# Block with sliding-window attention and a gated MLP: one tile for a stack's queries, one for its keys, in place of one for each half of the tokens

## The chip, the cores and the metric

One NeuronCore of a Trainium2 chip. The metric is the device time of one execution in microseconds, as the median of several runs. Each kernel also leaves one profiled execution, on which all the traces rest: the instructions of TensorE (PE, its weight loads PEld), VectorE (DVE), ScalarE (ACT), GpSimd (POOL) and the DMA queue of SyncE (SP), with their waits.

## The reference

Sequence S = 2048, width D = 640, all float32. The block is attention and then a gated MLP, each behind a layer norm and with a residual; the change touches the attention alone.

```python
H = 32; Dh = D // H; W = 256                       # Dh = 20
q, k, v = split(layernorm(x) @ wqkv)               # [H, S, Dh] each
scores = einsum("bhqd,bhkd->bhqk", q, k) * Dh ** -0.5
mask = (i - j >= 0) & (i - j < W)                  # query i, key j
p = softmax(where(mask, scores, -1e9))
h = x + (einsum("bhqk,bhkd->bhqd", p, v)) @ wo
z1, z2 = split(gelu(layernorm(h) @ w_in)); z2 = layernorm(z2)
h2 = h + (z1 * (w_sp @ z2 + b_sp)) @ w_out
```

Each query sees itself and the 255 keys before it. A block of 128 keys meets the 384 queries that begin with it; a block of 128 queries meets the 384 keys that end with it.

## The kernel before

**Stages.** First layer norm and the values (`vgemm`), then the query and key projections (`qk_item`) with the first maxima between them (the dense stage, to about 238 us), then the sliding attention in *units* (238 to about 457 us), the output projection, and the MLP.

**Stacks.** 32 heads are worked in 8 stacks of 4 heads. Queries and keys are split into three bf16 parts each, so that six products of parts stand for one float32 product; the six products are stacked along the contraction: 6 x 20 = 120 rows. Rows 120 to 122 hold ones on the side of the keys, and on the side of the queries the three bf16 parts of minus the row maximum, so that the same matmul with 123 rows yields score minus maximum. The projections write the parts to DRAM (`qk_d`, laid out by half of the heads, part, half of the tokens b, then rows, heads and 1024 tokens), and `load_stack` (L326 to L344) brings a stack back into SBUF with 24 DMAs: for each half b of the tokens, each of six products j and each side a (0 queries, 1 keys), 20 rows of 4 heads x 1024 tokens, 160 KB. A stack has a *slot* of two tiles of 16 KB a partition; three slots (0 and 1 of their own, 2 inside the buffer xb) are used in turn, `g % 3`. In the code before, tile b of a slot holds queries and keys of token half b, `p (a h t)`: so a row of one load is one run of 8 KB in SBUF. `slot_ap` views the tiles as bf16 for the matmuls, `slot_w` as float32 words of two tokens for the DMAs and memsets.

**Units.** Unit u is stack g = u // 16, key block kb = u % 16; NU = 128. In the loop over s (L788), unit s's scores (`score_item`), the maxima of unit s + 18 (`max_item`, LEAD = 18) and the PV products of unit s - 2 (`pv_item`) are interleaved head by head, for hh in 0 to 3.

- `max_item` (L359): scores of one head for 128 queries, without the maximum, in four strips of 32 queries (`tile_position` puts strip j on its own 32 columns of the array), each against the 288 keys that it can see (L373). Three PSUM banks (`ring[1]`) are used in turn; DVE takes the masked maximum of the bank (L383). Units below 18, in the dense stage, use one matmul of 128 queries and up to 384 keys (L377). After eight units, `max_rows` transposes the maxima on PE (L389), splits them into bf16 parts on DVE and POOL (L392 to L396), stores them (L398) and loads them into rows 120 to 122 of the queries (L400).
- `score_item` (L405): four strips of 32 keys against 288 queries each (L426) into one of three other banks; ACT takes the exponential (L429, in the last units L431), POOL zeroes what the window excludes (L433, L436).
- `pv_item` (L439): 16 matmuls (L454), copies from PSUM by ACT (L473) or DVE (L475), a store (L476).

**Where the halves meet.** A strip whose moving tokens lie on both sides of token 1024 takes them from two tiles, so `tokens` (L346) cuts it, and each piece becomes a matmul with a weight load of its own. That is so for maxima of query blocks 8 and 9 and for scores of key blocks 6 and 7 of every stack.

**Loads in time.** `load_stack(G)` starts when stack G - 2's scores start and issues one load in even units and two in odd ones, so it is spread over that stack's 16 units, with half 0 ahead of half 1 (for stack 0: queries ahead of keys). Stack G's maxima start in the last two of these 16 units with half 0; half 1 is first needed in key block 6 of stack G - 1.

**Order.** SP's, PE's, DVE's and ACT's instructions run in the order of the program throughout the attention; POOL's from unit 13 on is planned by the framework with a simulated time, and so is a part of the gate stage. Semaphores and waits follow from the tiles that each instruction reads and writes.

Of the kernel before, what the change touches and what calls it, by code (L numbers as in the profile page):

```python
# [7 lines left out]
F32 = mybir.dt.float32  # L8
# [7 lines left out]
P = 128  # L16
# [18 lines left out]
def block_kernel(ctx, tc, x, xt, wqk, wv, wo, w_in, wsp, bsp, w_out, out):  # L35
# [226 lines left out]
    with ExitStack() as ab:  # L262
# [19 lines left out]

        def add_slot(i, halves):

            slot_ap[i] = [h.bitcast(BF16).rearrange("p (a h t) -> p a h t", a=2, h=4) for h in halves]
            slot_w[i] = [h.bitcast(F32).rearrange("p (a h t) -> p a h t", a=2, h=4) for h in halves]

        add_slot(0, s0)
        add_slot(2, [h[:, :2 * S] for h in xb])
# [36 lines left out]
        def load_stack(g):  # L326


            st = slot_w[g % 3]
            if g < 2:  # L330
                for h in st:
                    nc.gpsimd.memset(h[96:P, 1], ONES)
            if g == 2:
                for h, ones in zip(st, slot_w[0]):
                    nc.sync.dma_start(h[120:123, 1], ones[120:123, 1])
                    yield
            parts = ((0, 0), (0, 1), (0, 2), (1, 0), (1, 1), (2, 0))
            loads = [(b, j, a) for b in range(2) for j in range(6) for a in range(2)]
            if g == 0:
                loads.sort(key=lambda load: load[2])  # L340
            for b, j, a in loads:
                src = qk_d[g // 4, parts[j][a], b, a * DH:(a + 1) * DH, g % 4 * 4:g % 4 * 4 + 4]
                nc.sync.dma_start(st[b][j:6 * DH:6, a], src)
                yield  # L344

        def tokens(st, rows, a, hh, t0, n):  # L346

            o = 0
            while o < n:
                c, t = divmod(t0 + o, S // 2)  # L350
                w = min(n - o, S // 2 - t)
                yield o, w, st[c][:rows, a, hh, t:t + w]
                o += w

        def one(st, rows, a, hh, t0, n):
            (_, _, x), = tokens(st, rows, a, hh, t0, n)
            return x

        def max_item(g, qb, hh, strips=True):  # L359

# [5 lines left out]
            if strips:  # L366
                skip = 32 if qb > 1 else 0
                if skip:
                    n, keep = 288, strip
                for j in range(4):  # L370
                    q0 = qb * P + 32 * j
                    for o, w, k in tokens(st, 120, 1, hh, lo + skip * j, n):
                        nc.tensor.matmul(ps[32 * j:32 * j + 32, o:o + w], one(st, 120, 0, hh, q0, 32), k,  # L373
                                         start=True, stop=True, tile_position=(0, 32 * j))
            else:
                for o, w, k in tokens(st, 120, 1, hh, lo, n):
                    nc.tensor.matmul(ps[:, o:o + w], one(st, 120, 0, hh, qb * P, P), k, start=True, stop=True)  # L377
            b, c = divmod(qb, 8)
            if c == 0 and hh == 0:
                m_cols[g, b] = tmp2.tile([P, 32], F32, tag="mcol", bufs=2, name=f"mcol{g}_{b}")  # L380
# [5 lines left out]
        def max_rows(g, b):  # L386
# [10 lines left out]
            rows = m_d[g, b]  # L397
            nc.sync.dma_start(rows.rearrange("a r c -> r a c"), m3.bitcast(F32))  # L398
            yield
            nc.sync.dma_start(slot_w[g % 3][b][120:123, 0], rows.rearrange("a (h r) c -> a h (r c)", h=4))  # L400
            yield

        p_tiles, pv_tiles = {}, {}
# [1 line left out]
        def score_item(u, hh):  # L405
# [14 lines left out]
            for i in range(4):  # L420
                k0 = kb * P + 32 * i
                b, e = 32 * i, min(n, 32 * i + 288)
                if NU - NT < u and 4 * (u - NU + NT - 1) + hh < 6:
                    b, e = 0, n
                for o, w, q in tokens(st, 123, 0, hh, kb * P + b, e - b):
                    nc.tensor.matmul(ps[32 * i:32 * i + 32, b + o:b + o + w], one(st, 123, 1, hh, k0, 32), q,  # L426
                                     start=True, stop=True, tile_position=(0, 32 * i))
            if u <= NU - NT:
                nc.scalar.activation(pt[:, hh, :n], ps[:, :n], AF.Exp, scale=SCALE)  # L429
            elif hh % 2:  # L430
# [1174 lines left out]
```

## Time and profile before

| | |
|---|---|
| median of 3 runs | 1100.6 us (1099.38 to 1101.7) |
| profiled execution, its own time | 1096.99 us |
| granted TensorE clock | 1.0 |
| matmuls, weight loads | 11045 each |
| PE, DVE, ACT, POOL busy in the whole span | 1073.5, 779.6, 603.7, 308.9 us |
| DMA: packets, bytes | 92293, 194.78 MB |

PE's busy time is made of matmuls whose ends are modelled, and they overlap, so a busy PE can still be waiting between starts. "Idle before" in a group is time in which that engine did nothing ahead of the group's instructions, with what ended it; "issue" is an end that no semaphore explains. In a name such as `bank<-slot,slot` the output stands ahead of the arrow; `slot,slot` are the two tiles of a slot, `xb,xb` those of slot 2.

### The profile page before, as it was taken

Reading aid. Unit: us, or ns where it says so; the run is one execution under the profiler, and the core shown is the slowest. Engines: PE = TensorE matmul, PEld = TensorE weight load, DVE = VectorE, ACT = ScalarE, POOL = GpSimd, SP = SyncE. Lnnn points to the kernel's source line nnn. Section 1 sums busy time; section 2 is a strip of 40 time slices with the busy share of each in tenths; the row PEclk is TensorE's granted clock in tenths of the full one; section 3 lists DMA queues with packets and bytes.
Section 4 is the critical chain, followed back from the end, with each engine's and each line's share of the span. In section 5 each row is a group of like instructions: output and inputs, shape, how many; then the busy total and the mean of one; then the engine's idle time right before and its main releaser. Section 6 shows DMA issues by size and latency. Waiting matters only on the chain.

```text
span 1095.3 us, 28703 instructions
## 1 busy us (share of the span) xinstructions
PE 1073.5 (98%) x11045; PEld 967.9 (88%) x11045; DVE 779.6 (71%) x2157; ACT 603.7 (55%) x1257; POOL 308.9 (28%) x446
## 2 busy tenths in 40 slices
PE   8999999999999999999999999999999999999998
PEld 8998886668888787699999998999999899999998
DVE  6643445779999997586677678656556899988674
ACT  4444433249989899766766557433358433333331
POOL 4414445668766677622200012000001000000000
PEclk9999999999999999999999999999999999999999
DMA  7834566465665565679845342242341567684542
GB/s 257 296 117 118 174 212 217 150 214 174 191 186 184 187 192 172 193 217 289 316 179 186 113 135 77 71 142 87 126 150 51 176 230 249 231 280 139 181 156 97
DMA packets 92293, 194.78 MB, mean 178 GB/s; under 512 B 11958, under 2 KB 46278, under 8 KB 88262
## 3 DMA queue, kind: packets, MB, share of 16 engines
q1 hardware_dynamic: 92156, 192.95, 54.0%
q8 instruction: 87, 1.43, 0.5%
q14 instruction: 50, 0.41, 0.1%
HBM read 127.90 MB, written 64.95 MB: 176 GB/s over the span
## 4 chain that ended last, share of the span: by engine, by line
PE 84%; DMA 4%; issue 4%; ACT 3%; DVE 2%; POOL 1%; SPq 1%; ACTq 0%; POOLq 0%; DVEq 0%
PE g L1217 23%; PE zb L1102 8%; PE pv L454 7%; PE bank L373 5%; PE bank L426 5%; PE qk L612 4%; PE qk L613 4%; PE qk L614 4%; PE out_x L1381 3%; PE zx L1042 2%; PE out_v L1381 2%; PE zv L1042 2%; PE zy L1042 1%; PE zw L1042 1%; PE bank L377 1%
## 5 line engine op out<-in xcount | busy, mean ns | idle before, releaser
L429 ACT ACTIVATE pt<-bank 128x384 f32<-128x384 f32 (+1 forms) x452 | 180.5, 486 | 14.5 <-PE bank L426 9.7
L1217 PE MATMUL g<-zl,aw 128*128 128x432 f32 x768 | 168.9, 357 | 1.0 <-ACT zl L864 1.0
L383 DVE CUSTOM_DVE_ANT_0 junk<-bank,strip 128x288 bf16<-128x288 f32 x392 | 155.8, 452 | 9.8 <-PE bank L373 5.6
L864 ACT ACTIVATE aw<-fx 128x512 fp32r<-128x512 f32 (+2 forms) x152 | 86.1, 587 | 128.4 <-DVE fx L858 53.6
L1217 PEld LDWEIGHTS g<-zl,aw 128*128 128x128 f32 x768 | 144.0, 188 | 7.4 <-ACT zl L864 1.4
L858 DVE TENSOR_TENSOR aw<-fx,aw 128x512 fp32r<-128x512 f32 (+2 forms) x152 | 95.7, 638 | 58.8 <-ACT aw L864 53.8
L454 PE MATMUL pv<-pt,v_sb 128*32 128x192 f32 (+3 forms) x1984 | 133.3, 322 | 2.9 <-POOL pt L433 1.2
L1217 PE MATMUL g<-ze,aw 128*128 128x432 f32 x576 | 132.6, 359 | 2.3 <-DVE row L858 2.3
L1217 PEld LDWEIGHTS g<-ze,aw 128*128 128x128 f32 x576 | 107.1, 188 | 9.0 <-DVE row L858 3.7
L433 POOL TENSOR_SCALAR_AFFINE_SELECT pt<-pt 128x512 f32<-128x512 f32 x128 | 82.6, 646 | 58.1 <-ACT pt L429 55.1
L426 PE MATMUL bank<-slot 123*32 123x288 bf16 (+8 forms) x1296 | 94.8, 273 | 1.0 <-ACT pt L429 0.6
L373 PE MATMUL bank<-slot 120*32 120x288 bf16 (+4 forms) x1248 | 91.6, 275 | 3.0 <-issue 2.8
L454 PEld LDWEIGHTS pv<-pt,v_sb 128*32 128x32 f32 x1984 | 64.1, 110 | 10.2 <-POOL pt L433 5.1
L436 POOL TENSOR_SCALAR_AFFINE_SELECT pt<-pt 128x512 f32<-128x512 f32 x112 | 71.0, 634 | 0.0
L426 PEld LDWEIGHTS <-slot 123*32 123x32 bf16 x1728 | 59.3, 96 | 11.5 <-issue 1.7
L858 DVE TENSOR_TENSOR row<-g,row 128x432 f32<-128x432 f32 x80 | 48.3, 603 | 21.3 <-PE g L1217 20.9
L373 PEld LDWEIGHTS <-slot 120*32 120x32 bf16 x1408 | 51.0, 95 | 14.0 <-issue 5.6
L383 DVE CUSTOM_DVE_ANT_0 junk<-bank,mask 128x384 bf16<-128x384 f32 (+2 forms) x120 | 51.4, 444 | 16.6 <-PE bank L377 14.7
L645 POOL TENSOR_TENSOR sg<-rest,sg 128x512 bf16<-128x512 f32 x39 | 45.6, 1169 | 57.7 <-ACT sg L644 45.2
L630 DVE TENSOR_TENSOR rest<-qk,std 128x512 f32<-128x512 f32 x36 | 24.8, 690 | 42.4 <-PE qk L614 41.2
L635 ACT ACTIVATE sg<-rest 128x512 bf16<-128x512 f32 x39 | 24.6, 631 | 54.1 <-DVE rest L630 52.3
L118 PE MATMUL wo_ps<-xb,xb 128*128 128x320 f32 x260 | 52.4, 311 | 0.5 <-DVE mvc L1496 0.5
(289 smaller groups left out, 2534.5 us busy)
## 6 DMA issues: line engine op xcount, KB each, us to landing
slot<-qk_d SPq DMA_DIRECT2D x144, 160.0 KB
fx<-wsp_in SPq DMA_DIRECT2D x32, 512.0 KB
qk_d<-sg SPq DMA_DIRECT2D x39, 384.0 KB
o_d<-ot SPq DMA_DIRECT2D x64, 128.0 KB
xb<-qk_d SPq DMA_DIRECT2D x48, 160.0 KB
fx<-hn_d SPq DMA_DIRECT2D x24, 320.0 KB
z_d<-row SPq DMA_DIRECT2D x16, 432.0 KB
g_d<-row SPq DMA_DIRECT2D x16, 432.0 KB
```

Source lines behind the costliest of these rows:

```text
L373: nc.tensor.matmul(ps[32 * j:32 * j + 32, o:o + w], one(st, 120, 0, hh, q0, 32), k, start=True, stop=True, tile_position=(0, 32 * j))
L383: nc.vector.tensor_tensor_reduce(out=junk[:, :n], in0=ps[:, :n], in1=keep, scale=1.0, scalar=NEG, op0=OP.add, op1=OP.max, accum_out=m_cols ...
L426: nc.tensor.matmul(ps[32 * i:32 * i + 32, b + o:b + o + w], one(st, 123, 1, hh, k0, 32), q, start=True, stop=True, tile_position=(0, 32 * i))
L429: nc.scalar.activation(pt[:, hh, :n], ps[:, :n], AF.Exp, scale=SCALE)
L433: nc.gpsimd.affine_select(out=pt[:, :, :P], in_=pt[:, :, :P], pattern=[[0, 4], [1, P]], base=0, channel_multiplier=-1, compare_op=OP.is_ge ...
L436: nc.gpsimd.affine_select(out=pt[:, :, 256:], in_=pt[:, :, 256:], pattern=[[0, 4], [-1, P]], base=-1, channel_multiplier=1, compare_op=OP. ...
L454: nc.tensor.matmul(ps[32 * hh:32 * hh + 32, a - 512 * c:b - 512 * c], v_sb[:, kb, v0:v0 + 32], pt[:, hh, a - kb * P:b - kb * P], start=fir ...
L858: (eng or nc.vector).tensor_tensor(out=out, in0=a, in1=b, op=op)
L864: nc.scalar.activation(out, a, AF.Copy)
L1042: nc.tensor.matmul(ps, a[x], b[:, y], start=start and m + x + y == 0, stop=stop and m == n - 1 and x == 1, skip_group_check=True)
L1102: nc.tensor.matmul(b[0][:, :HF], a[:, x, kk], win2[0][:, y, kk, h * HF:(h + 1) * HF], start=kk + x + y == 0, stop=kk == KD - 1 and x == 1)
L1217: nc.tensor.matmul(ps, w[m][:, x, k], zc[k][m][:, y], start=start and k + x + y == 0, stop=stop and k == 3 and x == 1, skip_group_check=True)
```

## The change

Tile 0 of a slot now holds the queries of all 2048 tokens and tile 1 the keys, `p (h t)`. So every strip is one matmul, `tokens` is gone, and `one` is a plain slice. The loads read the same parts of `qk_d` in the same order, but a row's four heads of 1024 tokens now land 4 KB apart in four runs of 2 KB. The rows with minus the maximum (L400) land in the same manner. The ones (rows 96 to 127 by memset for slots 0 and 1, copied for slot 2) are written in two pieces of two heads of the keys' tile, where they were one piece for each half.

```diff
--- before.py
+++ after.py
@@ -282,8 +282,8 @@

         def add_slot(i, halves):

-            slot_ap[i] = [h.bitcast(BF16).rearrange("p (a h t) -> p a h t", a=2, h=4) for h in halves]
-            slot_w[i] = [h.bitcast(F32).rearrange("p (a h t) -> p a h t", a=2, h=4) for h in halves]
+            slot_ap[i] = [h.bitcast(BF16).rearrange("p (h t) -> p h t", h=4) for h in halves]
+            slot_w[i] = [h.bitcast(F32).rearrange("p (h t) -> p h t", h=4) for h in halves]

         add_slot(0, s0)
         add_slot(2, [h[:, :2 * S] for h in xb])
@@ -328,11 +328,11 @@

             st = slot_w[g % 3]
             if g < 2:
-                for h in st:
-                    nc.gpsimd.memset(h[96:P, 1], ONES)
+                for b in range(2):
+                    nc.gpsimd.memset(st[1][96:P, 2 * b:2 * b + 2], ONES)
             if g == 2:
-                for h, ones in zip(st, slot_w[0]):
-                    nc.sync.dma_start(h[120:123, 1], ones[120:123, 1])
+                for b in range(2):
+                    nc.sync.dma_start(st[1][120:123, 2 * b:2 * b + 2], slot_w[0][1][120:123, 2 * b:2 * b + 2])
                     yield
             parts = ((0, 0), (0, 1), (0, 2), (1, 0), (1, 1), (2, 0))
             loads = [(b, j, a) for b in range(2) for j in range(6) for a in range(2)]
@@ -340,21 +340,11 @@
                 loads.sort(key=lambda load: load[2])
             for b, j, a in loads:
                 src = qk_d[g // 4, parts[j][a], b, a * DH:(a + 1) * DH, g % 4 * 4:g % 4 * 4 + 4]
-                nc.sync.dma_start(st[b][j:6 * DH:6, a], src)
+                nc.sync.dma_start(st[a][j:6 * DH:6, :, b * S // 4:(b + 1) * S // 4], src)
                 yield

-        def tokens(st, rows, a, hh, t0, n):
-
-            o = 0
-            while o < n:
-                c, t = divmod(t0 + o, S // 2)
-                w = min(n - o, S // 2 - t)
-                yield o, w, st[c][:rows, a, hh, t:t + w]
-                o += w
-
         def one(st, rows, a, hh, t0, n):
-            (_, _, x), = tokens(st, rows, a, hh, t0, n)
-            return x
+            return st[a][:rows, hh, t0:t0 + n]

         def max_item(g, qb, hh, strips=True):

@@ -369,12 +359,12 @@
                     n, keep = 288, strip
                 for j in range(4):
                     q0 = qb * P + 32 * j
-                    for o, w, k in tokens(st, 120, 1, hh, lo + skip * j, n):
-                        nc.tensor.matmul(ps[32 * j:32 * j + 32, o:o + w], one(st, 120, 0, hh, q0, 32), k,
-                                         start=True, stop=True, tile_position=(0, 32 * j))
+                    nc.tensor.matmul(ps[32 * j:32 * j + 32, :n], one(st, 120, 0, hh, q0, 32),
+                                     one(st, 120, 1, hh, lo + skip * j, n),
+                                     start=True, stop=True, tile_position=(0, 32 * j))
             else:
-                for o, w, k in tokens(st, 120, 1, hh, lo, n):
-                    nc.tensor.matmul(ps[:, o:o + w], one(st, 120, 0, hh, qb * P, P), k, start=True, stop=True)
+                nc.tensor.matmul(ps[:, :n], one(st, 120, 0, hh, qb * P, P), one(st, 120, 1, hh, lo, n),
+                                 start=True, stop=True)
             b, c = divmod(qb, 8)
             if c == 0 and hh == 0:
                 m_cols[g, b] = tmp2.tile([P, 32], F32, tag="mcol", bufs=2, name=f"mcol{g}_{b}")
@@ -397,7 +387,8 @@
             rows = m_d[g, b]
             nc.sync.dma_start(rows.rearrange("a r c -> r a c"), m3.bitcast(F32))
             yield
-            nc.sync.dma_start(slot_w[g % 3][b][120:123, 0], rows.rearrange("a (h r) c -> a h (r c)", h=4))
+            nc.sync.dma_start(slot_w[g % 3][0][120:123, :, b * S // 4:(b + 1) * S // 4],
+                              rows.rearrange("a (h r) c -> a h (r c)", h=4))
             yield

         p_tiles, pv_tiles = {}, {}
@@ -422,9 +413,9 @@
                 b, e = 32 * i, min(n, 32 * i + 288)
                 if NU - NT < u and 4 * (u - NU + NT - 1) + hh < 6:
                     b, e = 0, n
-                for o, w, q in tokens(st, 123, 0, hh, kb * P + b, e - b):
-                    nc.tensor.matmul(ps[32 * i:32 * i + 32, b + o:b + o + w], one(st, 123, 1, hh, k0, 32), q,
-                                     start=True, stop=True, tile_position=(0, 32 * i))
+                nc.tensor.matmul(ps[32 * i:32 * i + 32, b:e], one(st, 123, 1, hh, k0, 32),
+                                 one(st, 123, 0, hh, kb * P + b, e - b),
+                                 start=True, stop=True, tile_position=(0, 32 * i))
             if u <= NU - NT:
                 nc.scalar.activation(pt[:, hh, :n], ps[:, :n], AF.Exp, scale=SCALE)
             elif hh % 2:
```

## The prediction

> **What bounds the kernel now.** I read the page first, then the windows view for the stage that the diff touches (units 0 to 112 of the sliding attention, 238 to 434 us, and the units behind them), then PE's waits inside that stage.
>
> ```profile
> span 1095.3 us, 28703 instructions
> ```
>
> ```profile
> 238.00:434.00 196.00, 190.01 (x5722) 160.92 (x5724) 183.84 (x934) 181.73 (x474) 139.97 (x241) 1.00 0.59 184
> 434.00:458.00 24.00, 22.00 (x543) 14.34 (x542) 9.86 (x14) 22.49 (x38) 20.49 (x32) 1.00 0.66 182
> ```
>
> ```profile
> PE bank L373 <- issue: 3.4, 5, 1.6
> ```
>
> The window rows list the length, then PE, PEld, DVE, ACT and POOL busy, the clock, the DMA share and GB/s. In the long stage PE is busy 190.0 of 196 us, DVE 183.8, ACT 181.7: three engines in step, so a saving on one is worth only what the other two leave. In the last units ACT holds 22.5 of 24 us, so PE's saving there counts nothing. Most of PE's idle time is "issue": it waits for nothing the profile shows; L373 alone has five such waits, 3.4 us.
>
> **What the change removes.** A matmul whose tokens cross 1024 was two, each with its own weight load.
>
> ```profile
> L426 PEld LDWEIGHTS <-slot 123*32 123x32 bf16 x1728 | 59.3, 96 | 11.5 <-issue 1.7
> L373 PEld LDWEIGHTS <-slot 120*32 120x32 bf16 x1408 | 51.0, 95 | 14.0 <-issue 5.6
> L373 PEld LDWEIGHTS <-xb 120*32 120x32 bf16 x576 | 20.7, 95 | 5.2 <-issue 1.6 <-DMA xb<-qk_d 0.2
> L426 PEld LDWEIGHTS <-xb 123*32 123x32 bf16 x576 | 20.0, 96 | 3.5 <-issue 0.7
> ```
>
> ```profile
> L377 PE MATMUL bank<-slot,slot x8: 231/258/285, 200.9 to 207.7; 120*128 120x256 bf16 x4, 120*128 120x128 bf16 x4
> ```
>
> Whole strips need 110 x 16 = 1760 maxima matmuls (L373) and 128 x 16 = 2048 score matmuls (L426); the rows give 1984 and 2304. So 224 + 256 + 8 (L377) = 488 matmuls and 488 weight loads go. They sit together: score blocks 6 and 7 of a stack and maxima blocks 8 and 9 of the next fall into the same two units (maxima run 18 units ahead, a stack has 16). Seven such pairs lie in the long stage.
>
> What a pair costs PE, from its timeline; then an ordinary half unit:
>
> ```profile
> 276.03 0.27 PE L373 MATMUL bank<-xb,xb 120*32 120x256 bf16 x2
> ...
> 279.27 0.22 PE L373 MATMUL bank<-xb,xb 120*32 120x128 bf16 x4
> ...
> 279.85 0.34 PE L373 MATMUL bank<-xb 120*32 120x288 bf16 x4
> ```
>
> ```profile
> 284.89 0.31 PE L373 MATMUL bank<-xb 120*32 120x288 bf16 x4
> ...
> 285.72 0.30 PE L373 MATMUL bank<-xb 120*32 120x288 bf16 x4
> ```
>
> The pair runs from 276.03 to 279.85, 3.82 us; four ordinary halves of 0.83 are 3.32. So 0.50 us a pair, 3.5 us for seven, if PE alone set the pace. There it does not. DVE in 276.4 to 281.1, by groups (the last column is idle time before them), and one row of its timeline:
>
> ```profile
> L383 DVE CUSTOM_DVE_ANT_0 junk<-bank,strip 128x288 bf16<-128x288 f32 x10 | 4.0, 442 | 0.0
> L383 DVE DVE_READ_ACCUMULATOR2_ANT mcol<- 128x1 f32 x10 | 0.7, 73 | 0.0
> L475 DVE COPY ot<-pv 128x256 f32<-128x256 f32 x1 | 0.4, 408 | 0.0
> L393 DVE SCALAR_TENSOR_TENSOR mr<-bank,m 32x128 f32<-32x128 f32 x1 | 0.3, 278 | 0.0
> L392 DVE TENSOR_SCALAR m<-bank 32x128 bf16<-32x128 f32 x1 | 0.3, 276 | 0.0
> ```
>
> ```profile
> 279.15 0.07 DVE L383 DVE_READ_ACCUMULATOR2_ANT mcol<- 128x1 f32 x1
> ```
>
> DVE is never idle there: in the same pair it also drains a PV copy (L475) and the maxima's transpose (L392, L393), and maxima have three banks. At 279.22 (279.15 + 0.07) DVE gives a bank back, at 279.27 PE's next maximum starts. PE is waiting for DVE, and a shorter strip would only wait longer. I take 0 for this term, by the nearest row; the ends are 0 and 3.5 us. Behind DVE, ACT's 181.7 us are next.
>
> What I do count are PE's stalls. One windows call over the seven pairs, each from DVE's first maximum of the first unit to the first one behind the pair, ends in the sum below; ahead of it two of the pairs and an ordinary stretch, behind it the stall in the first of them, and the page's queue of instructions (packets, MB, share).
>
> ```profile
> 303.30:309.10 5.80, 4.18 (x171) 3.70 (x165) 4.06 (x21) 3.88 (x10) 3.04 (x6) 1.00 0.60 181
> 389.60:393.50 3.90, 3.90 (x170) 3.67 (x162) 3.83 (x20) 3.75 (x10) 3.04 (x6) 1.00 0.63 211
> 281.10:286.90 5.80, 5.80 (x178) 5.16 (x172) 5.72 (x29) 5.80 (x16) 4.15 (x7) 1.00 0.66 205
> ```
>
> ```profile
> sum 31.50, PE 28.59 PEld 25.67 DVE 27.98 ACT 26.65 POOL 22.32; mean PE 4.08 PEld 3.67 DVE 4.00 ACT 3.81 POOL 3.19
> ```
>
> ```profile
> 308.09 0.24 PE L373 MATMUL bank<-slot 120*32 120x192 bf16 x1 [1.60 <-issue]
> ```
>
> ```profile
> q8 instruction: 87, 1.43, 0.5%
> ```
>
> A pair without a stall takes 3.90 us; seven took 31.5, so 31.5 - 27.3 = 4.2 us are stalls (PE's idle time shows 2.9 of it, since the ends of matmuls are modelled). In a pair PE starts 170 matmuls in 3.9 us, 43.6 per us; in the ordinary stretch 178 in 5.8, 30.7. The page counts 11045 matmuls and as many weight loads, so each of the 87 instruction transfers carries some 254 PE instructions; at two a matmul they last 254 / 87.2 = 2.9 us in a pair and 254 / 61.4 = 4.1 us elsewhere. My reading, an inference: in a split pair the queue of instructions falls behind. Elsewhere it does so too, more rarely: PE is idle 6.0 us in the whole stage, 3.1 of it outside the pairs, so 0.5 us for 27.3 ordinary us, and by the same 4.2 : 2.9 some 0.7. The pairs then keep 0.7 of their 4.2: **3.5 us gained** (ends: 0, if stalls only move, and 4.2).
>
> [...]
>
> The eight split maxima of the dense stage: 8 x 0.258 = 2.1 us at most, 0 at least (they overlap their neighbours); I take 0.3, near the lower end.
>
> **What it adds.** The 192 loads keep their order, queue and 160 KB, but land in four runs of 2 KB a row where there was one of 8 KB; the 16 row loads of L400 likewise. No wait is added.
>
> ```profile
> L343 SPq DMA_DIRECT2D slot<-qk_d x144: 694/722/1977, 145.9 to 409.7; - x144
> ```
>
> ```profile
> 456.48 0.59 SPq L229 DMA_DIRECT2D inv<-o_d  x1
> ```
>
> ```profile
> SPq L476 <- ACT pt L429: 10.2, 21, 4.0
> ```
>
> ```profile
> 315.00:317.00 2.00, 2.00 (x64) 1.68 (x60) 1.97 (x11) 1.98 (x6) 1.67 (x4) 1.00 0.35 107
> 102.00:103.50 1.50, 1.50 (x9) 1.18 (x8) 0.69 (x1) 0.08 (x1) 1.17 (x1) 1.00 0.82 165
> ```
>
> Issue on SP: 24 x 0.72 = 17.3 us of a stack's 28 (196 us for 112 units). The reciprocals' load, whose source lies in short pieces, takes 0.59, so more pieces are not seen to cost more; I take 0.72, with ends of 0.59 and twice 0.72. SP spends time waiting (10.2 us for one cause alone), and loads come early: in the L373 rows above one matmul waited for one, 0.2 us.
>
> On the DMA engines: two us in which stack loads prevail give 107 / (16 x 0.35) = 19.1 GB/s an engine, a stretch of 2 KB broadcast rows 165 / (16 x 0.82) = 12.6. At the worse end a stack's 24 x 160 KB = 3.9 MB in 28 us (140 GB/s) would take 0.69 of the engines instead of 0.46, and the stage's 0.59 would become 0.82: not full. I take 0. The memsets and the copy of ones keep number and size: 0.
>
> Waits: reads of one half and writes of the other now share a tile. If an access were tracked by its outer bounds, maxima would wait for loads of the other half. The trace has the same pattern already:
>
> ```profile
> 22.08 0.74 ACT L537 ACTIVATE xa<-xt_t 128x640 fp32r<-128x640 f32 x1 [0.93 <-DVE xt_t L535]
> 22.11 0.31 PE L560 MATMUL v<-slot,xa 128*128 128x320 f32 x1
> ```
>
> The matmuls read one token block of xa while ACT, earlier in the program, writes the next block in five strided pieces between theirs, and they do not wait. So 0.
>
> Sum: 3.5 + 0.3 + 0 = 3.8 us. The profiled execution took 1096.99 us (span 1095.3), which would become 1093.2; it lies 3.6 below the median of three runs, 1100.6, so for the median I predict **1096.8**.
>
> **The rivals.**
> 1. *The stalls only move* (no change). For it: the waits of L373 for "issue" are spread over the stage, DVE is full in a pair, and 488 of 11045 matmuls are few. Then 0 to 1 us: 1100.1.
> 2. *PE's shorter strips count as well.* Banks free earlier before and behind the pair: 3.8 + 3.5 = 7.3, 1093.3. Against it: DVE's idle 0.0.
> 3. *Slower, by the instruction queue.* Four times the packets stand ahead of an instruction transfer, at up to 0.82 of the engines. It decides from the point at which an ordinary stretch's 4.1 us no longer cover a transfer: then the pairs' 4.2 us in 31.5 come all through the 196, 26 us, less the 9 there now: up to 17 slower. A beginning of it, 3 to 8 us, is likelier: 1105.
> 4. *Slower, by SP.* Beside 24 loads a stack has 8 stores and 4 row transfers; at 0.59 at most 7.1 us. It decides above (28 - 7.1) / 24 = 0.87 us a load. At 1.2 a stack slips 7.9 us, six stacks 47, less some 10 of lead (a second half is first used six units behind its last load): 1138.
>
> The change surely does what it says: the counts of L373 and L426 follow from it.
>
> **How the numbers follow.** Forecast 0.50 (its own range 1094 to 1098.4); rival 1 0.27; rival 2 0.09; rival 3 0.09; rival 4 0.05. A measurement of this kernel tells about 0.2%, 2.2 us, from no change. Faster: the forecast less its upper edge, and rival 2: 0.58. Same: rival 1 and that edge: 0.28. Slower: 0.14. The range runs from below rival 2's time, 1092, to the lower half of rival 3, 1104.5; rival 4 and the rest of 3 stay out.
>
> **What would show it.** Right: 1760 and 2048 weight loads; pairs at 3.9 us, most without "issue" idle; DVE's idle in them still 0.0; L343's issue near 0.72; loads hardly waited for. Wrong: pairs under 3.7 us (rival 2), as much "issue" idle as before (rival 1) or more (rival 3), L343 above 0.87 with matmuls waiting for qk_d (rival 4). Two orders are planned and not written out, POOL's from unit 13 on and part of the gate stage; they may move by a us either way, which I can't read here.

## The result and the profile after: 12% slower

| | before | after |
|---|---|---|
| median | 1101.15 us (6 runs, 1096.9 to 1102.87) | 1234.42 us (6 runs, 1232.66 to 1238.56) |
| ratio, 95% interval | | 1.122 (1.1192 to 1.1248) |
| span of the profiled execution | 1095.3 us | 1231.7 us |
| matmuls | 11045 | 10557 |

The prediction said 1096.8 us and gave slower 0.14. The 488 matmuls did go, and the time went up by 133 us.

I read the page of after first: the span, PE's line, the granted clock in 40 slices, and the packets.

```profile
span 1231.7 us, 27722 instructions
PE 1109.9 (90%) x10557; PEld 989.5 (80%) x10557; DVE 783.4 (64%) x2157; ACT 606.1 (49%) x1257; POOL 311.9 (25%) x446
...
PEclk9999987798888888879999999999999999999999
...
DMA packets 103953, 194.72 MB, mean 158 GB/s; under 512 B 11958, under 2 KB 46278, under 8 KB 103814
```

Two things stand out. PE is *busier* than before (1109.9 us against 1073.5) with fewer matmuls, and the clock is down in slices 6 to 18 (all but one) and nowhere else. These slices are the dense stage behind the first maxima and the attention. So the windows view is cut there: from 173 us to the first score (237 us before, 291 after), and from there to the last score's end (457 and 596). First before, then after:

```profile
173.00:237.00 64.00, 64.00 (x307) 40.16 (x309) 46.23 (x163) 18.19 (x29) 39.55 (x37) 1.00 0.53 178
237.00:457.00 220.00, 212.01 (x6270) 174.94 (x6270) 193.44 (x949) 204.42 (x511) 160.10 (x273) 1.00 0.60 183
```

```profile
173.00:291.00 118.00, 81.38 (x296) 49.57 (x295) 46.78 (x163) 19.07 (x31) 41.85 (x38) 0.80 0.33 107
291.00:596.00 305.00, 232.80 (x5797) 188.46 (x5797) 198.87 (x951) 206.33 (x510) 160.61 (x272) 0.88 0.43 129
```

The dense stage lost 54 us: 36.6 of PE idle (118 - 81.4) and 17.4 of PE longer busy at a clock of 0.80. The attention lost 85: idle rose from 8.0 to 72.2, busy by 20.8 at 0.88. That is 139; behind the attention after is 2.6 us *faster* (635.7 against 638.3). The DMA share fell from 0.60 to 0.43, so the engines of the transfers are not what is full. What PE waits for stands in the waits view (us in total, times, longest):

```profile
PE bank L362 <- DMA slot<-qk_d: 41.6, 8, 6.1
PE bank L366 <- DMA slot<-qk_d: 34.3, 8, 6.7
PE bank L362 <- DMA xb<-qk_d: 20.1, 3, 9.8
PE bank L416 <- DMA slot<-m_d: 6.7, 2, 5.7
```

Few waits, each long: the first three rows are loads of a stack, 96 us in 19 waits, where before no maximum waited for one longer than 0.2 us. The timeline shows the longest, with SP's loads of the same tile ahead of it:

```profile
319.12 1.58 SPq L343 DMA_DIRECT2D xb<-qk_d  x2
320.80 0.42 SPq L467 DMA_DIRECT2D o_d<-ot  x1
321.27 1.58 SPq L343 DMA_DIRECT2D xb<-qk_d  x2
```

```profile
326.17 0.30 PE L362 MATMUL bank<-xb,xb 120*32 120x128 bf16 x4 [9.76 <-DMA xb<-qk_d]
```

`120x128` is block 0 of a stack: it reads the first 128 keys, half 0 of the tokens. The issue of half 0's twelve loads had ended 15 us before; PE stood idle until the *last* loads, half 1's, had been issued, and 3.3 us more (their issue ended at 321.27 + 1.58 = 322.85).

Which loads does it wait for? The built program says so by its semaphores. Loads of a stack are numbered in order of issue, 0 to 11 for half 0, 12 to 23 for half 1, odd ones keys. For stack 3 (those loads that a semaphore names; the count waited for includes earlier loads on the same semaphore):

```
kernel                       first matmul that waits               waits for loads
before                       block 0, head 0                       4, 7, 8, 9, 10, 11
                             block 8 (token 1024)                  16, 18 to 23
after                        block 0, head 0                       8, 9, 10, 11, 17, 19, 21
                             block 1, head 0                       23
                             block 8                               16, 20, 22
```

After the change, block 0 waits for three key loads of half 1, and block 1 for the last. Neither reads a byte of them. Half 1's query loads, written in the same way, are not waited for early here, where a strip reads 32 queries; in stack 1, whose maxima read 128 queries at a time, block 0 waits for them too (12, 14 and 16). So the width of the read matters as well; why is not shown. In return the last key load counts as overwriting what these maxima read, so SP waits for PE: in stacks 3 to 7 its issue ended 4.9 to 5.3 us *behind* the start of DVE's first maximum of the stack. So a stack's first two units run in step with the queue: loads are issued and land, a unit runs and lets the next load out, that lands, the next unit runs. The trace has two waits in each of stacks 3 to 7, of 5.3 to 6.1 and 4.5 to 5.1 us.

### The profile page after: what moved, and what is told of

It reads as the page before. It is cut to its first block, busy times and chain, and to the rows that moved or that the text cites. A ratio compares the mean times of both kernels' runs of the same rounds, so it can differ in the third digit from the quotient of the medians.

```text
span 1231.7 us, 27722 instructions
## 1 busy us (share of the span) xinstructions
PE 1109.9 (90%) x10557; PEld 989.5 (80%) x10557; DVE 783.4 (64%) x2157; ACT 606.1 (49%) x1257; POOL 311.9 (25%) x446
## 2 busy tenths in 40 slices
DMA packets 103953, 194.72 MB, mean 158 GB/s; under 512 B 11958, under 2 KB 46278, under 8 KB 103814
## 4 chain that ended last, share of the span: by engine, by line
PE 67%; DMA 10%; issue 6%; ACT 5%; DVE 5%; SPq 4%; POOL 3%; POOLq 0%; DVEq 0%; ACTq 0%
PE g L1208 20%; PE wo_ps L118 4%; PE pv L445 4%; PE zb L1093 4%; PE bank L362 4%; DMA slot<-qk_d 4%; PE bank L416 3%; PE out_x L1372 3%; PE qk L603 3%; PE qk L604 3%; PE qk L605 3%; SPq L343 2%; PE zx L1033 2%; PE out_v L1372 2%; PE zv L1033 2%
## 5 line engine op out<-in xcount | busy, mean ns | idle before, releaser
L445 PE MATMUL pv<-pt,v_sb 128*32 128x192 f32 (+3 forms) x1984 | 145.3, 347 | 1.7 <-POOL pt L427 0.8
L362 PE MATMUL bank<-slot,slot 120*32 120x288 bf16 (+2 forms) x1248 | 98.9, 304 | 42.2 <-DMA slot<-qk_d 41.6
L416 PE MATMUL bank<-slot,slot 123*32 123x288 bf16 (+5 forms) x1296 | 101.6, 297 | 7.4 <-DMA slot<-m_d 6.7
L362 PEld LDWEIGHTS <-slot 120*32 120x32 bf16 x1248 | 49.8, 102 | 56.8 <-DMA slot<-qk_d 33.7
L445 PEld LDWEIGHTS pv<-pt,v_sb 128*32 128x32 f32 x1984 | 70.3, 117 | 8.2 <-POOL pt L424 3.7
L416 PEld LDWEIGHTS <-slot 123*32 123x32 bf16 x1536 | 56.9, 102 | 20.8 <-DMA slot<-m_d 7.4
L366 PE MATMUL bank<-slot,slot 120*128 120x384 bf16 (+2 forms) x72 | 26.6, 370 | 36.6 <-DMA slot<-qk_d 34.3
L362 PE MATMUL bank<-xb,xb 120*32 120x288 bf16 (+2 forms) x512 | 40.8, 303 | 20.3 <-DMA xb<-qk_d 20.1
```

What stands on the lines that cost most here:

```text
L362: nc.tensor.matmul(ps[32 * j:32 * j + 32, :n], one(st, 120, 0, hh, q0, 32), one(st, 120, 1, hh, lo + skip * j, n), start=True, stop=True, ...
L416: nc.tensor.matmul(ps[32 * i:32 * i + 32, b:e], one(st, 123, 1, hh, k0, 32), one(st, 123, 0, hh, kb * P + b, e - b), start=True, stop=True ...
L445: nc.tensor.matmul(ps[32 * hh:32 * hh + 32, a - 512 * c:b - 512 * c], v_sb[:, kb, v0:v0 + 32], pt[:, hh, a - kb * P:b - kb * P], start=fir ...
```

## The experiments

The framework keeps account of what each instruction reads and writes and derives the waits from it; below this is called the tracker. Three theories. **A**: waits that the tracker adds between the halves of a shared tile cost the time. **B**: the runs of 2 KB do (more packets, longer issue). **C**: sharing a tile costs by itself. (The expectation of the second run gives the letter C to something narrower, a tracker that compares outer bounds inside a row; its 1100 us did not come.)

### Which part costs: runs, shared tile, partition step

**Runs alone.** Halves in their own tiles as before, the heads outermost, so that a row lands in four runs:

```diff
-rearrange("p (a h t) -> p a h t", a=2, h=4)
+rearrange("p (h a t) -> p a h t", a=2, h=4)
```

> The kernel before with one edit: inside a half's tile the heads stand outermost (p (h a t)), so every row of a load lands in four runs of 2 KB, as after the change, but tiles, strips and matmuls are those of before. Theory A (added waits between the halves of a shared tile cost the time, the runs nothing): 1096 to 1104 us, the same as before, the load's issue at about 0.77 us, PE's first maxima of a stack without long waits. Theory B (the 2 KB runs themselves, by four times the packets or a longer issue, cost the time): near 1234.

Measured: 1108.61 us, ratio 1.0075 (1.0052 to 1.0098). B is not the cause of 133 us, but my 1096 to 1104 was wrong too: the runs cost 8 us. Maxima now wait for loads, shortly; the first two rows of the waits view:

```profile
PE bank L373 <- DMA slot<-qk_d: 4.6, 5, 1.7
PE bank L373 <- issue: 2.5, 3, 1.9
```

More on that below.

**Shared tile, 8 KB runs.** Queries in one tile, keys in the other, but the halves apart, strips cut as before:

```diff
-rearrange("p (h t) -> p h t", h=4)
+rearrange("p (b h t) -> p b h t", b=2, h=4)
...
-nc.sync.dma_start(st[a][j:6 * DH:6, :, b * S // 4:(b + 1) * S // 4], src)
+nc.sync.dma_start(st[a][j:6 * DH:6, b], src)
```

> The changed layout as to which tile holds what (queries in one, keys in the other), but inside it the halves stand apart (p (b h t)): a row of a load is one run of 8 KB as before, and strips are cut at token 1024 as before, so all 11045 matmuls are back. Theory A, in its form that a write with a partition step of 6 is taken to touch the whole row: 1210 to 1245, the first maximum of a stack waiting for loads of the other half as after the change. Theory B (runs of 2 KB): about 1100. A third theory C (a tracker that compares outer bounds inside a row only): about 1100 too, since the halves' bounds are apart here.

Measured: 1228.5 us (one run), with 11045 matmuls, 92293 packets and these windows:

```profile
173.00:291.00 118.00, 77.45 (x306) 47.82 (x304) 48.70 (x164) 20.06 (x32) 43.24 (x39) 0.83 0.34 111
291.00:596.00 305.00, 242.17 (x6390) 199.05 (x6390) 206.60 (x962) 206.86 (x513) 160.77 (x272) 0.88 0.45 137
```

The same loss, idle and clock, without a single run of 2 KB. Its first maxima wait for loads 17, 19 and 21, as after the change.

**No partition step.** A load's 20 rows on neighbouring partitions (`j * DH:(j + 1) * DH`) instead of every sixth one; first in the changed kernel, then with the shared tile and 8 KB runs, then in the kernel before.

> The changed kernel with one edit: the 20 rows of a load go to 20 neighbouring partitions (j * 20 up) instead of every sixth one; queries and keys get the same order of rows, so the sums are the same. Theory A predicts by which access is compared exactly: head 0 of a stack's first block waits for the right loads only, heads 1 to 3 still for those of the other half, since without the step a row's four runs are taken by their outer bounds, which start 2 KB behind the first head: 1200 to 1240. If the step alone is to blame: about 1097. Theory B: 1234.

> Both edits together: queries and keys each in one tile, halves apart in it (one run of 8 KB a row, strips cut at 1024), and 20 neighbouring partitions a load. Theory A: every maximum waits for its own half's loads alone, as before: 1096 to 1106, so a shared tile costs nothing by itself. That sharing a tile costs by itself, however it is laid out: 1210 to 1245. If 20 neighbouring partitions make a load slower on the DMA engines, loads take longer from issue to landing and some maxima wait: 1105 to 1120.

> The kernel before with one edit: the 20 rows of a load go to 20 neighbouring partitions instead of every sixth one; tiles, strips and order of before. If the 25 us of the run with a shared tile and neighbouring partitions come from the neighbouring partitions (its 8 KB packets took 506 ns in the median instead of 309): 1115 to 1130. If they come from sharing the tile: 1097 to 1103.

Measured: 1253.49 (one run), above its range; 1124.83, ratio 1.0222 (1.0165 to 1.0279), above its ranges for theory A; 1127.58, ratio 1.0265 (1.0219 to 1.031), as expected. In the first, head 0 of block 0 waits for half 0 alone, and head 1 for 17, 19 and 21: without the step a row's runs are taken by their outer bounds, which begin behind head 0's first 1024 tokens. In the second every maximum waits for its own half, and 104 of the added us (1228.5 less 1124.8) are gone; what is left is also there in the third, which shares nothing. C falls. The remaining 25 to 30 us are the neighbouring partitions' own, seen in one stretch of before and of the second:

```profile
245.00:420.00 175.00, 170.00 (x5210) 145.16 (x5203) 166.11 (x850) 162.72 (x425) 125.68 (x219) 1.00 0.60 187
```

```profile
245.00:420.00 175.00, 153.76 (x4460) 130.17 (x4459) 145.74 (x736) 143.22 (x369) 111.53 (x191) 0.96 0.65 164
```

More of the engines' time (0.65 against 0.60) moves less (164 GB/s against 187): from 260 to 400 us, the same 8 KB packets took 506 ns in the median instead of 309. Why the packets took longer is not shown: these loads were also issued in half the time (335 ns in the median instead of 722).

### By what feature: the type of the view

Step and runs mattered only because the tracker of reads and writes didn't see through them. One feature was left: the DMAs write through `slot_w`, words of float32, and the matmuls read through `slot_ap`, bf16. The first edit is made in the changed kernel, the same one in the run of 1228.5 us.

```diff
-nc.sync.dma_start(st[a][j:6 * DH:6, :, b * S // 4:(b + 1) * S // 4], src)
+nc.sync.dma_start(slot_ap[g % 3][a][j:6 * DH:6, :, b * S // 2:(b + 1) * S // 2], src.bitcast(BF16))
```

(and the row load of minus the maximum likewise)

> The changed kernel with two lines edited: the loads and the rows of minus the maximum are written through the bf16 view of the slot, through which the matmuls read it, instead of the float32 view of words of two tokens; the bytes, the places and the 2 KB runs are the same. In the built program every maximum then waits for its own half's loads alone, as before the change. If the added waits are the whole of the 134 us but for what 2 KB runs cost (7.5 us in the run of the change without its waits): 1100 to 1112. If something else of the change costs (a shared tile, whole strips): above 1120.

> The run with a shared tile and 8 KB runs (1228 us), with the same edit: writes through the bf16 view. Partition step of 6, shared tiles, strips cut and runs of 8 KB stay. If the type of the view is what made the tracker lose the step: 1096 to 1104, as before the change. If the step itself costs, whatever the view: 1210 to 1245.

Measured: **1109.01 us**, ratio 1.0068 (1.0046 to 1.009), from 1234; and **1100.87**, ratio 1.0008 (0.9989 to 1.0028), from 1228.5. Block 0 of stack 3 waits for 4 and 7 to 11 in both, as before. Of the 96 us of waits for loads, the waits view of the first has these rows left for maxima and scores (a row with m_d or o_d at L362 is a load too, since maxima read nothing of either):

```profile
PE bank L362 <- issue: 2.6, 3, 2.1
PE bank L362 <- DMA xb<-qk_d: 1.7, 1, 1.7
PE bank L416 <- DMA slot<-m_d: 1.6, 2, 1.0
PE bank L416 <- DMA xb<-m_d: 1.5, 2, 0.8
...
PE bank L362 <- DMA o_d<-ot: 1.2, 1, 1.2
PE bank L362 <- DMA slot<-m_d: 1.1, 1, 1.1
...
PE bank L362 <- DMA slot<-qk_d: 1.1, 1, 1.1
PE bank L362 <- DMA xb<-m_d: 1.0, 1, 1.0
```

The edit moves and resizes no transfer: packets (103953), bytes and the loads' issue (0.77 us) stay. It takes out the added waits alone, and with them 125 and 128 us; in the first the granted clock is 1.0 again. So A holds: a strided write through a view of another element type was taken to touch the other half as well, for reads of 128 tokens and more.

### What the removed matmuls are worth

```diff
-            o = 0
-            while o < n:
-                c, t = divmod(t0 + o, S // 2)
-                w = min(n - o, S // 2 - t)
-                yield o, w, st[c][:rows, a, hh, t:t + w]
-                o += w
+            c, t = divmod(t0, S // 2)
+            if t + n > S // 2:
+                c, t = 1, 0
+            yield 0, n, st[c][:rows, a, hh, t:t + n]
```

A strip that would cross token 1024 thus takes all its tokens from half 1, so these two kernels leave out these strips' products with the tokens ahead of 1024 and serve for the time alone.

> The kernel before with one edit: a strip that would cross token 1024 is taken whole from the start of half 1 instead of being cut, so it multiplies other tokens than it should; everything else, tiles, 8 KB runs, loads and their waits, stays. 488 matmuls and weight loads go, as in the change. It measures by itself what the prediction summed to 3.8 us (1097 against 1101). The prediction's first rival says 0 to 1 us, its second 7.3 us; the two cut twins gave 3 and 10 us, in kernels with more stalls than this one.

> The same edit on top of the first run's layout (halves in their own tiles, but a row of a load in four runs of 2 KB): the change as the prediction saw it, with all its parts but the added waits. If the prediction was wrong in the waits alone: 1097. If 2 KB runs cost here the 8 us that they cost by themselves in the first run: 1100 to 1106, so the forecast would have been wrong even without the waits.

Measured: 1093.97 us, ratio 0.9948 (0.9928 to 0.9968), so 5.7 us faster (3.5 to 7.9); on top of the 2 KB runs 1109.17, ratio 1.0068 (1.0049 to 1.0088), above both of its expectations. The windows of the first over the seven pairs of units (the first, the third, the last and the sum):

```profile
248.89:252.76 3.87, 3.79 (x110) 3.13 (x105) 3.84 (x20) 3.78 (x10) 3.79 (x8) 1.00 0.42 112
...
304.75:308.62 3.87, 3.87 (x110) 3.36 (x106) 3.83 (x18) 3.39 (x8) 2.50 (x5) 1.00 0.63 192
...
417.91:421.87 3.96, 3.88 (x110) 3.14 (x105) 3.92 (x18) 3.52 (x8) 2.91 (x6) 1.00 1.00 340
sum 27.18, PE 26.74 PEld 22.27 DVE 26.93 ACT 24.95 POOL 19.32; mean PE 3.82 PEld 3.18 DVE 3.85 ACT 3.56 POOL 2.76
```

All seven pairs take what the unstalled ones took before: 3.87 to 3.96 us, 27.2 in all against 31.5. The stalls are gone, and no pair is shorter than 3.87: DVE sets that, with 3.83 to 3.92 us of work in each. In this one execution other stalls took the 4 us back, and these are waits for loads, though the loads are those of before in runs of 8 KB:

```profile
PE bank L371 <- DMA slot<-qk_d: 3.8, 3, 2.6
```

All three of PE's stalls above 0.6 us in the attention end at the first maximum of a stack's second half (at 304.40, 334.02 and 389.93). With PE faster, the loads are no longer early enough: a limit that the forecast did not have, and one that eats into its gain. The gain itself rests on the twelve runs.

### Other ways around the waits

These came before the type of the view was found. The first only issues the changed kernel's loads earlier:

```diff
-            for _ in range(1 + s % 2 if s >= NT else 2 * (s > 1)):
+            for _ in range(2 * (s > 1)):
```

> The changed kernel with one edit: two loads a unit all through (the changed kernel issues one and two in turn), so all 24 loads of a stack are out by unit 12 of 16 and no load is issued beside the stack's first maxima. The waits stay in the program; they should find their loads landed. Theory A: the attention's own loss goes (first to last score took 219 us before and 303 after the change, so 84 us), the dense stage's loss of 54 us stays, since stack 0's and 1's loads are not moved: 1145 to 1165. If instead the transfers are too slow for the units, however early they are issued: above 1200.

Measured: 1210.15 (one run), a miss. From first to last score 281 us (288.5 to 569.1) instead of 303. The loads were early in the program, not on the chip: 24 issues of 0.77 us are 18.5 us, and twelve units of 1.75 us are 21. The last load's issue ended only 3.7 to 4.7 us ahead of the stack's first maximum, in all six stacks: about the time that a load took to land above (3.3 us).

The other five store `qk_d` without halves, so that a load brings all 2048 tokens and no second half comes later:

```diff
-    qk_d = dram.tile([2, 3, 2, 2 * DH, H // 2, S // 4], F32, name="qk_d")
+    qk_d = dram.tile([2, 3, 2 * DH, H // 2, S // 2], F32, name="qk_d")
...
-                nc.sync.dma_start(st[a][j:6 * DH:6, :, b * S // 4:(b + 1) * S // 4], src)
+                nc.sync.dma_start(st[a][j:6 * DH:6], src)
...
-            for _ in range(1 + s % 2 if s >= NT else 2 * (s > 1)):
+            for _ in range(1 if s >= NT else 2 * (s > 1)):
```

> The changed kernel with a layout of qk_d in DRAM without the halves (rows, heads, 2048 tokens), so a load is one run of 16 KB a row and 320 KB in all, 12 loads a stack, one a unit in its first twelve units; no write of one half beside reads of the other is left, except the rows of minus the maximum, which still land in runs of 2 KB. Stack 0's keys are loaded ahead of its first maxima, with twelve instead of six steps of the dense stage between. Whole strips as in the changed kernel. Theory A: all of the loss goes but for up to 7 us that scores wait for the rows of minus the maximum (6.7 us after the change): 1093 to 1108. If whole strips themselves cost (a shared tile, or matmuls with two operands' tiles in another order): above 1110.

Measured: 1156.95, ratio 1.0519 (1.0495 to 1.0543). Theory A had 1093 to 1108. The rows of minus the maximum were waited for as expected, but four times as long, and the first maxima of five stacks stood for 13.5 us more:

```profile
PE bank L416 <- DMA slot<-m_d: 20.4, 6, 6.6
...
PE bank L416 <- DMA xb<-m_d: 5.6, 2, 3.5
```

```diff
-            nc.sync.dma_start(slot_w[g % 3][0][120:123, :, b * S // 4:(b + 1) * S // 4],
-                              rows.rearrange("a (h r) c -> a h (r c)", h=4))
+            for hh in range(4):
+                nc.sync.dma_start(slot_w[g % 3][0][120:123, hh, b * S // 4:(b + 1) * S // 4],
+                                  rows.rearrange("a (h r) c -> a h (r c)", h=4)[:, hh])
```

> As the run with whole rows, and the rows of minus the maximum are loaded head by head, four DMAs of one run a row where there was one of four, so no access is left whose runs interleave with another half's. Theory A: a stack's first scores no longer wait for the rows of the second half: 0 to 7 us less than with whole rows alone, 1090 to 1100. If SP's issues matter (24 more a stack's 16 units... 6 more DMAs a stack at some 0.3 us): up to 3 us more.

Measured: 1135.91, ratio 1.0303 (1.0274 to 1.0332), not 1090 to 1100. None of these waits are left; 3.2 to 5.8 us ahead of each stack are, for its last load. All tokens of a stack are needed 14 units after its slot is free, where before half of them had eight units more. So, loads further ahead:

```diff
-            for _ in range(1 if s >= NT else 2 * (s > 1)):
+            for _ in range(1 + s % 2 if s >= NT else 2 * (s > 1)):
```

> As the run with rows by head, with loads further ahead: one and two in turn (so twelve loads are out by unit 8 instead of 12), and 24 steps of the dense stage instead of 12 between stack 0's loads of keys and its first maxima (one step in four is left out between the maxima in return). In the run with rows by head PE stood idle 6.7 us before stack 0's first maximum and 3.2 to 5.8 us before each later stack's, 32 us in seven places. Theory A (what is left there is landing time of loads issued too close to their first reader): 1094 to 1104. If whole strips or the layout cost by themselves: still above 1120.

Measured: 1109.25, ratio 1.0109 (1.008 to 1.0137), not 1094 to 1104. No wait for a load above 0.7 us is left, but 13.6 us of "issue". Two variants of it: even spacing (`1 + (s % 4 == 3)` a unit), and loads of two heads (24 of 160 KB, runs of 8 KB, `2 + s % 2` a unit):

> As the run with loads further ahead (16 KB runs, 12 loads), with loads spread: one a unit and two in every fourth, out by unit 9 instead of 7, so five a four units instead of six. Theory A1 (packet size): as there, 1105 to 1113. Theory A2 (rate): fewer stalls for instructions, 1100 to 1106. If loads land too late again, the first maximum of a stack waits for them as in the run with rows by head: above 1115.

> As the run with loads further ahead, with 24 loads of 160 KB a stack again (two heads, all tokens, one run of 8 KB a row as before the change) in place of 12 of 320 KB; two and three a unit in turn, out by unit 9. The run with loads further ahead lost 16.6 us in stalls of PE above 0.4 us, nearly all without a semaphore, each of which ended 1.4 to 1.7 us behind the end of one of PE's instruction transfers. Theory A1 (bursts of 16 KB packets hold up the instruction transfers): with packets of 8 KB the stalls shrink to the 5 us of before: 1094 to 1102. Theory A2 (the rate of the loads counts, not the size of a packet): stalls as there, 1105 to 1115.

Measured: 1111.7, ratio 1.0131 (1.0104 to 1.0158), with 9.6 us of waits of the maxima for DMAs come back; and 1133.27, ratio 1.0327 (1.0291 to 1.0364). The latter is bound by the issue again:

```profile
L344 SPq DMA_DIRECT2D slot<-qk_d x144: 707/708/1397, 146.8 to 439.9; - x144
```

24 x 0.71 = 17 of the 17.5 us that ten units have; PE stands 3.8 to 7.7 us ahead of each of stacks 2 to 7. So neither A1 nor A2 is settled by these, and what makes up the 12 us of the kernel with loads ahead stays open.

Three of the five have a twin whose strips are cut at token 1024 again, for scores and whole maxima as for these:

```diff
-                    nc.tensor.matmul(ps[32 * j:32 * j + 32, :n], one(st, 120, 0, hh, q0, 32),
-                                     one(st, 120, 1, hh, lo + skip * j, n),
+                    for o, e in pieces(lo + skip * j, n):
+                        nc.tensor.matmul(ps[32 * j:32 * j + 32, o:e], one(st, 120, 0, hh, q0, 32),
+                                         one(st, 120, 1, hh, lo + skip * j + o, e - o),
```

> As the run before it, with one edit: strips that cross token 1024 are cut there again, each piece a matmul with its own weight load, all 11045 as before the change. Layout, loads and waits stay. This measures what the whole strips are worth by themselves. The prediction's forecast: 3.8 us slower than with whole strips. Its first rival (stalls only move): 0 to 1 us. Its second (PE's shorter strips count too): 7.3 us.

> As the run before it, with strips cut at token 1024 again (11045 matmuls). The prediction's forecast: 3.8 us slower than with whole strips; its first rival: 0 to 1 us; its second: 7.3 us.

> As the run before it, with strips cut at token 1024 again. By the last two pairs of runs whole strips were worth 3 and 10 us. If what they save is stalls for instructions (976 PE instructions less), the worth follows the stalls: 2 to 5 us where stalls are few, near 10 where they are many.

Measured: 1138.97, 1119.11 and 1140.42, that is 3, 10 and 7 us above their twins (the 3 us within the spread of the runs), of kernels that are themselves slower than before. The pair of 10 us shows where they lie. The seven pairs' sum in the kernel with loads ahead, and in its cut twin:

```profile
sum 32.61, PE 28.43 PEld 22.13 DVE 27.43 ACT 26.10 POOL 22.44; mean PE 4.06 PEld 3.16 DVE 3.92 ACT 3.73 POOL 3.21
```

```profile
sum 43.26, PE 29.79 PEld 26.49 DVE 28.28 ACT 26.40 POOL 22.76; mean PE 4.26 PEld 3.78 DVE 4.04 ACT 3.77 POOL 3.25
```

The pairs differ by 10.7 us in these two executions, the medians by 9.9: as far as one execution each can show, it all lies there. No version beats the kernel before. The only faster one works on other tokens.

## Why the prediction was wrong, step by step

- **"No wait is added", "Waits: ... So 0."** The step that failed: 0 stood for some 125 us (1234.4 less 1109.0). I saw the risk (an access tracked by its outer bounds) and put it aside by one row pair, ACT writing xa in strided pieces beside PE's reads. That evidence is good for what it shows, but there both accesses have 4-byte elements; here a float32 view is written and a bf16 view read. I treated it as a term of the sum and not as a rival with a price; a price was at hand: a load issued beside its reader keeps PE for issue and landing (4.5 to 6.1 us a wait in stacks 3 to 7), twice a stack and, as the waits view has it, eight times in the dense stage.
- **"I take 0.72 ... I take 0" for the 2 KB runs.** Failed as well, and by itself it would have turned the sign: the change without its waits is 7.5 us slower (5.4 to 9.7 with half tiles and other tokens, 5.1 to 9.9 with views of one type), not 3.8 faster. The issue grew little, and the row loads' issue nearly threefold. Before, then after with views of one type:

```profile
L400 SPq DMA_DIRECT2D slot<-m_d x12: 266/271/442, 215.0 to 438.1; - x12
```

```profile
L343 SPq DMA_DIRECT2D slot<-qk_d x144: 748/770/1868, 145.4 to 420.4; - x144
...
L390 SPq DMA_DIRECT2D slot<-m_d x12: 708/732/748, 213.7 to 444.8; - x12
```

  A stack's 24 loads and two row loads then cost 24 x 0.05 + 2 x 0.46 = 2.1 us more of SP in 28. Rival 4 was this mechanism, and its threshold of 0.87 us a load was too high: I set against it SP's time (7.1 us of other work), not the lead of a half's last load over its first reader. "Loads come early" was read off one wait of 0.2 us, which shows that they came in time, not by how much. Worked out from the traces, from the issue's end of loads 11 and 23 to the start of DVE's first maximum of that half (stacks 2 to 7, us):

```
                        half 0                          half 1
before                  6.5 5.7 5.8 6.8 6.2 7.8         8.9 5.8 5.1 4.9 6.3 6.7
2 KB runs alone         6.3 3.6 3.1 4.1 3.5 4.0         8.6 4.0 4.2 4.0 3.1 3.7
after, one type         4.5 4.0 4.2 3.8 3.1 4.2         5.8 4.1 3.0 4.4 3.2 3.9
whole strips, 8 KB      6.5 5.7 4.3 4.3 3.6 4.1         7.5 3.9 4.9 4.8 3.9 4.4
shared, 8 KB, one type  7.1 8.0 9.1 6.6 8.6 7.5         11.1 8.7 7.0 7.0 6.5 4.6
```

  Before, there were 5 to 9 us; with the longer issues mostly 3 to 4, about the time in which a load landed above (3.3 us), and short waits for loads and row loads appear: those of maxima and scores are 6.4 us with 2 KB runs alone and 9.2 in the third row. They are absent in the first and the last row, where all leads but one are 4.9 us or more. The fourth row is between: its maxima wait 4.9 us, without a longer issue, since PE comes sooner. That the lead is the whole of the 7.5 us is argued, not shown: no run changed the issue time alone.
- **3.5 us of "issue" stalls in the pairs, 0 for PE's own 0.50 us a pair.** Both right in mechanism and nearly in size: 31.5 became 27.2, so 4.3 us, and the floor of 3.87 stayed DVE's. The whole, 3.8 us, was measured as 5.7 (3.5 to 7.9); the 0.3 us of the dense stage no run tells apart. With 2 KB runs it is not seen: 1.0068 against 1.0075 with strips cut.
- **The queue of instructions as the cause of those stalls.** Supported. In the kernel with loads ahead, PE's stalls over 0.6 us that end in "issue", from 250 to 420 us, against the end of the last transfer ahead of them on the page's instruction queue q8:

```
stall ends    258.29 264.76 269.89 295.42 343.82 373.89 380.39 415.05   (and 327.27)
transfer ends 256.74 263.39 268.14 293.90 342.39 372.30 379.02 413.62   (324.44)
difference      1.55   1.37   1.75   1.52   1.43   1.59   1.37   1.43   (2.83)
```

  All eight resume 1.4 to 1.75 us behind a transfer's end, where transfers end some 4.7 us apart (the ninth, in brackets, the view puts down to a DMA); before, the stalls that end at 308.09 and 421.08 do so by 1.39 and 1.27 (transfers to 306.70 and 419.81). And the stalls go where 488 of the matmuls go (the seven pairs' 31.5 us became 27.2).
- **Rival 1** (stalls only move) came true in the single profile, though as waits for loads and not for instructions, and not in the medians. **Rival 2** (7.3 us) fell: no pair is under 3.87. **Rival 3** did not happen: PE's waits for "issue" in the attention are 4.7 us with 2 KB runs alone and 4.8 before. **Rival 4** did, in small.

## What to carry to other kernels

When two uses that had a tile each come to share one, list what each access waits for in the built program first: a strided write through a view of another element type than the read's lost the distinction between the halves for all but the narrowest reads, and one type on both sides brought 125 us back. A trace row shows exactness only for the kind of access in it. Where a queue issues loads just in time, count the lead of the last load over its first reader, not the queue's busy share: 5 to 9 us of lead hid every load here, 3 to 4 no longer did. Work taken off the reader shortens that lead too: half 1's was 4.9 to 8.9 us before and 3.9 to 7.5 with whole strips.

## What was not expected of the hardware

**The clock followed the waits.** 38 of the 139 us are PE busy for longer, not idle. One row of L362 by its line: median 287 ns, longest 448.

```profile
L362 PE MATMUL bank<-slot,slot x1248: 264/287/448, 291.0 to 562.3; 120*32 120x288 bf16 x160, 120*32 120x256 bf16 x10, 120*32 120x128 bf16 x9
```

The waits of maxima for loads in the attention are 4.5 to 9.8 us. Around the longest (316.41 to 326.17) the clock is 1.00 from 310 to 321 us, 0.50 from 322 to 331, so for 5 us of PE's work behind the wait too, and 1.00 again from 332. A shorter wait went with a lower clock as well: in the kernel with loads ahead, two pairs with one stall each, of 2.20 us (clock 0.78) and of 1.52 us (1.00):

```profile
340.65:348.29 7.64, 5.44 (x108) 4.03 (x103) 4.27 (x19) 3.96 (x10) 3.25 (x7) 0.78 0.68 245
371.40:376.83 5.43, 3.91 (x110) 3.08 (x105) 3.92 (x20) 3.67 (x10) 3.08 (x6) 1.00 0.72 263
```

So a wait of 2.2 us went with another 1.5 in PE's time here (5.44 against 3.91), and one of 1.5 with none. That is no threshold: with whole strips in the halves' own tiles, a wait of 2.6 us (to 334.02) left the clock at 1.00 from 300 to 350 us.

**The load to neighbouring partitions issued faster, and its packets took longer.** In the kernel before, the load on 20 neighbouring partitions was issued in 0.33 us instead of 0.72, and the kernel lost 2.65%, with packets of 496 ns instead of 309.
